# Chunked attention with a mixture of experts on one core: the second product turned for two batches, seven products one step sooner

## The chip, the core and the metric

The kernel runs on one core of a Trainium2 chip. What is measured is the time of one execution on the device, in microseconds (us). Three runs of the kernel before gave 1075.25, 1075.27 and 1075.59 us; their median is 1075.27.

## What is computed

Four batches of 768 tokens, 8 heads of 64: each chunk of 32 tokens attends to 8 memory keys and to its neighbourhood (16 tokens to the left, 8 to the right). The result, 3072 tokens x 512 features, goes through four experts, each with two matrix products, and the experts' outputs are added with routing weights:

```python
for c in range(nc):                       # chunks of 32
    k_full = np.concatenate([mem_k, k_ctx], axis=2)
    scores = scale * np.matmul(q_c, k_full.transpose(0, 1, 3, 2))
    a = np.exp(scores - np.max(scores, axis=-1, keepdims=True))
    a = a / (np.sum(a, axis=-1, keepdims=True) + 1e-09)
    out[:, :, c_start:c_end] = np.matmul(a, v_full)
...
p = domain_probs / (domain_probs.sum(-1, keepdims=True) + 1e-09)
for e in range(E):                        # 4 experts, w1: 512x1024, w2: 1024x512
    h = np.maximum(x @ w1[e], 0.0)
    out += p[:, e:e + 1] * (h @ w2[e])
```

## The kernel before

**Steps.** There are 16 steps, n = 4 x batch + expert. A step computes both products of one expert for the 768 tokens of one batch, in two halves of 384 tokens (SG). All operands are fp32 numbers split into a high and a low part; a product of two is three passes of TensorE (high x high, high x low, low x high). The splitting is a cast on ScalarE and a subtraction on VectorE or GpSimd (`parts_of`, L531).

**Seven products.** Where a product is cut into 2 x 2 blocks, `combine_x`, `make_pair` and `make2_combined` build sums of blocks so that seven block products do instead of eight. The first product has this form from step 1 on (classes `Pair` and `Full`: `one_two`, `six`, `five`, `seven`, `four`, `three`). Its seven products are done for four pairs of feature blocks p = 0 to 3, each a group of 6 matmuls of 384 columns (L860), with a weight block as the stationary operand and tokens as the columns. The second product is plain in steps 0 to 4 (`Tokens`, L822: 6 token tiles x 8 feature blocks x 3 passes = 144 matmuls of 512 columns, L840), and has seven products from step 5 (`Halves`, L1047: the hidden activations are the stationary operand, the columns are 256 output features, 3 token tiles per product; L1084). What it adds up in PSUM, `add_up` (L805) multiplies by the routing weight p_e of each token, a per-partition scalar there, and adds to `acc` in SBUF: on VectorE, with a first copy on ScalarE.

**Three stages.** The program is written in three plans. The first covers the attention of batch 0 and part of step 0; the second steps 0 to 4; the third steps 5 to 15. While a batch's experts run, the attention of the next batch is computed in between (`attend`, `window`), eight units a batch. In the second stage the first-layer weights of a step are loaded, combined, split, used, and stored in HBM (`make_pair`, L685); w2 likewise (`make2`); the combined w2 blocks (`make2_combined`, L746) are made from raw tiles and only stored. In the third stage nothing is split any more: `Stream` (L989) brings stored weights through a ring of 9 tiles of 512 KB, in order of use, and sends a load when a tile comes free.

**What sets the order.** `Plan` (L112) records every operation with its engine, a time from a formula, and the tiles it reads and writes. TensorE's order is as written; on the other engines and on SyncE, which issues all DMAs in order, a list scheduler orders by due time. `run` (L185) tries 100 variants (600 in the first stage), replays each, and keeps the best by TensorE's end, or by the last end in the last stage. Operations written with `join` may go to VectorE or GpSimd. `after` (L217) hands engine times on to the next plan; there SyncE may start up to 4 us ahead of it. At the end of the second stage the pools of raw tiles, weights and hidden tiles are closed and the ring is laid over them (`open_fin`, L423).

Of the kernel before, what the change touches and what calls it, by code (L numbers as in the profile page):

```python
# [38 lines left out]


# [19 lines left out]
DMA_ISSUE, DMA_FIRST, DMA_RATE = 0.45, 2.0, 345e3  # L60
ENGINES = ("PE", "ACT", "DVE", "POOL", "SP")
# [21 lines left out]
class Tile:  # L83
# [4 lines left out]
    def __init__(self, make, parts):  # L88
        self.make, self.parts, self._ap, self.ops = make, parts, None, []
        self.held, self.behind, self.born = False, None, 0  # L90
# [10 lines left out]
class Op:  # L101
# [3 lines left out]
    def __init__(self, engine, time, fn, birth, two, bytes_, index):  # L105
# [3 lines left out]
        self.floor = 0.0  # L109


class Plan:  # L112
# [21 lines left out]
    def slot(self, tag, aps, parts=1):  # L134

        t = self.tile(None, tag, len(aps), parts)
        t._ap = t.behind._ap if t.behind else aps[len(self.tags[tag]) - 1]
        return t
# [17 lines left out]
    def add(self, engine, time, fn, reads=(), writes=(), two=False, bytes_=0, other=None):  # L156
# [8 lines left out]
        for key in reads + writes:  # L165
            op.floor = max(op.floor, self.ends.get(key, 0.0))
            t = key[0] if isinstance(key, tuple) else key
            if isinstance(t, Tile):
                assert not getattr(t, "gone", False), "a tile is used after its place was given away"
                if t.behind is not None:  # L170
                    op.deps.update(t.behind.ops)
                    t.behind.gone = True
# [12 lines left out]
    def run(self, turns=TURNS, seed=1, last=False):  # L185

        ops, self.last = self.ops, last
# [83 lines left out]
    def replay(self, order, seed):  # L271
# [3 lines left out]
        dma = pool_to = dve_to = 0.0  # L275
# [21 lines left out]
        self.done = free  # L297
        return max(end) if self.last else free["PE"]

    def schedule(self, bias, ways):  # L300
# [10 lines left out]
        dma = pool_to = dve_to = drift = 0.0  # L311
# [77 lines left out]
PIECES = [[(0, KW, 0)], [(0, KW, CH)], [(0, NM, MEM), (NM, KW, 2 * CH + NM)]]  # L389
KORDER = [f for p in range(NP2) for f in (p, p + NP2)]  # L390
# [3 lines left out]
def tile_chunked_attention_moe(ctx: ExitStack, tc: tile.TileContext, qk, v, probs, w1, w2, out):  # L394
# [6 lines left out]
    opool = ctx.enter_context(tc.tile_pool(name="opool", bufs=6))  # L401
    mid_ctx = ExitStack()
    raw = mid_ctx.enter_context(tc.tile_pool(name="raw", bufs=3))
# [73 lines left out]
    psum_e = const.tile([P, NT, 1], F32, name="psum_e")  # L477

# [68 lines left out]
    def window(us, i, last=False):  # L547
# [71 lines left out]
        def inverted():  # L619
# [4 lines left out]
        dve(lambda: nc.vector.tensor_tensor(  # L624
            out=s_sb.ap, in0=s_sb.ap, in1=sm.ap.broadcast_to([UQ, H, KW]), op=ALU.mult), n_s, [sm], [s_sb])
# [12 lines left out]
    def combine_x(first):  # L638
# [6 lines left out]
        t3 = new(lambda: late["sb"], [P, h2 * SG + 256], "s_t", 1)  # L645
        t3_ap = lambda: t3.ap[:, 0:n_x].rearrange("p (a b) -> p a b", a=h2)

        def put(dst, name, i, x, key):
            at = slice(i * h2, (i + 1) * h2)
            parts_of(lambda: dst[0][:, at], lambda: dst[1][:, at], x, n_x, [key], (name, i, 0), (name, i, 1))  # L650

        def sub(out, x, y, reads, writes):
            join(out, x, y, ALU.subtract, n_x, reads, writes)

        if not first:
            put(xa, "xa", 0, lambda: b11, k11)
            put(xa, "xa", 1, lambda: b21, k21)
        sub(t3_ap, lambda: b22, lambda: b12, [k22, k12], [t3])
        if not first:
            put(xb, "xb", 1, lambda: b22, k22)  # L660
        sub(lambda: b12, lambda: b12, lambda: b11, [k11], [k12])
        sub(lambda: b22, lambda: b22, lambda: b12, [k12], [k22])
        put(xc, "xc", 1, lambda: b22, k22)
        put(xc, "xc", 0, lambda: b12, k12)
        put(xc, "xc", 2, t3_ap, t3)
        sub(lambda: b21, lambda: b21, lambda: b22, [k22], [k21])
        put(xb, "xb", 0, lambda: b21, k21)
# [11 lines left out]
    def want_pair(n, p):  # L679
        r = new(lambda: late["sb"], [P, 2 * DM], "raw_pair", 2, parts=2)  # L680
        for i, f in enumerate((p + NH, p)):
            dma(lambda i=i: r.ap[:, i * DM:(i + 1) * DM], lambda f=f: w1[n % E, f], P * DM * 4, [], [(r, i)])
# [829 lines left out]
```

## Time and profile before

| | us |
|---|---|
| median of three runs | 1075.27 |
| the profiled execution | 1075.24 |
| its span, first to last instruction | 1073.5 |
| TensorE busy | 1057.2 |
| VectorE / ScalarE / GpSimd busy | 757.1 / 651.5 / 305.2 |

The page of the profile also shows a mean DMA rate of 267 GB/s, and three of 40 slices in which TensorE is busy for less than nine tenths: the first (6), the fifteenth around 380 us (8), where the second stage ends, and the last (8). Matmuls overlap in the records, so the time from one start to the next tells what one costs.

### The profile page before, as it was taken

What the parts mean: (1) busy time and instruction counts of PE and PEld (TensorE: products, weight loads), DVE (VectorE), ACT (ScalarE), POOL (GpSimd) and SP (SyncE); (2) the same over time, 40 slices, a digit from 0 to 9 for tenths busy, and PEclk for the clock granted to TensorE, in tenths of its full rate; (3) what the DMA queues carried; (4) which work ended last, traced back from release to release, by engine and by line L of the source; (5) the groups of instructions that cost most, each with busy time, mean ns of one, the idle gap of its engine ahead of it and who ended that gap; (6) DMA issues with size and microseconds to landing.
All of it is one profiled execution on the core that took longest, in us unless ns stands there. A gap on an engine that the chain in (4) does not pass through costs nothing.

```text
span 1073.5 us, 20388 instructions
## 1 busy us (share of the span) xinstructions
PE 1057.2 (98%) x7438; PEld 1010.7 (94%) x7438; DVE 757.1 (71%) x1366; ACT 651.5 (61%) x1654; POOL 305.2 (28%) x302
## 2 busy tenths in 40 slices
PE   6999999999999989999999999999999999999998
PEld 6988988989889889999999999999999999999998
DVE  5956876757786348869698865858689654747474
ACT  5836885657665657585865867657592645435261
POOL 3321524627253214243352612112010221303020
PEclk8999999999999999999999999999999999999999
DMA  8553696967877499999998978878777977877783
GB/s 266 188 185 125 248 386 225 393 227 298 316 254 292 144 342 315 307 351 323 336 327 301 345 242 279 255 238 273 239 241 240 303 252 234 267 233 248 247 258 136
DMA packets 169364, 286.61 MB, mean 267 GB/s; under 512 B 14128, under 2 KB 108336, under 8 KB 169264
## 3 DMA queue, kind: packets, MB, share of 16 engines
q1 hardware_dynamic: 169264, 285.31, 77.8%
q8 instruction: 59, 0.97, 0.4%
q14 instruction: 41, 0.34, 0.1%
HBM read 216.06 MB, written 69.21 MB: 266 GB/s over the span
## 4 chain that ended last, share of the span: by engine, by line
PE 97%; DVE 1%; ACT 1%; DMA 1%; POOL 0%; issue 0%; SPq 0%; POOLq 0%; ACTq 0%; DVEq 0%
PE a_ps L860 24%; PE a_ps L1084 18%; PE moe_ps L860 18%; PE moe_ps L840 14%; PE moe_ps L1084 13%; PE moe_ps L794 3%; PE s_ps L560 2%; PE x_ps L579 2%; PE att_ps L1249 1%; PE x_ps L1268 1%; PE x_ps L1148 1%; DMA ring<-k 0%; PE att_ps L1177 0%; ACT s_sb L615 0%; DMA t<-s_t 0%
## 5 line engine op out<-in xcount | busy, mean ns | idle before, releaser
L840 PE MATMUL moe_ps<-w,h_hi 128*128 128x512 f32 x480 | 149.6, 393 | 0.0
L521 DVE TENSOR_TENSOR u<-moe_ps,u 128x384 f32<-128x384 f32 x120 | 66.5, 555 | 79.3 <-PE moe_ps L860 61.1
L840 PEld LDWEIGHTS moe_ps<-w,h_hi 128*128 128x128 f32 x480 | 88.9, 188 | 18.7
L505 ACT ACTIVATE u<-u 128x384 f32<-128x384 f32 x132 | 68.8, 523 | 60.7 <-DVE u L521 60.5
L503 ACT COPY u<-a_ps 128x384 f32<-128x384 f32 x120 | 57.3, 477 | 73.2 <-PE a_ps L860 69.5
L522 POOL TENSOR_TENSOR u<-u,u 128x384 f32<-128x384 f32 x33 | 40.1, 1217 | 198.5 <-DVE us L521 194.7
L840 PE MATMUL moe_ps<-w,h_lo 128*128 128x512 f32 x240 | 93.8, 391 | 0.0
L521 DVE TENSOR_TENSOR A_lo<-u,A_hi 128x384 fp32r<-128x384 f32 x119 | 76.2, 649 | 18.6 <-ACT A_hi L503 18.4
L814 DVE SCALAR_TENSOR_TENSOR acc<-moe_ps,pr,acc 128x256 f32<-128x256 f32 (+1 forms) x109 | 56.7, 523 | 36.6 <-PE moe_ps L1084 21.8
L1084 PE MATMUL moe_ps<-ring,A_hi 128*128 128x256 f32 x440 | 80.9, 283 | 0.0
L814 DVE SCALAR_TENSOR_TENSOR acc<-a_ps,pr,acc 128x256 f32<-128x256 f32 x116 | 55.7, 480 | 35.3 <-PE a_ps L1084 34.5
L633 DVE STREAM_TRANSPOSE aT<-band 32x256 f32<-32x256 f32 x168 | 73.0, 435 | 5.6 <-ACT band L503 2.6
L860 PE MATMUL a_ps<-xc_hi,ring 128*128 128x384 f32 x352 | 75.6, 336 | 0.0
L522 POOL TENSOR_TENSOR u<-u,us 128x384 f32<-128x384 f32 x40 | 48.9, 1224 | 84.8 <-DVE A_lo L521 49.4
L1084 PEld LDWEIGHTS moe_ps<-ring,A_hi 128*128 128x128 f32 x440 | 69.0, 191 | 0.0
L503 ACT CAST A_hi<-u 128x384 fp32r<-128x384 f32 x132 | 67.4, 513 | 0.9
L1084 PE MATMUL a_ps<-ring,Sa_hi 128*128 128x256 f32 x352 | 65.4, 285 | 0.0
L615 ACT ACTIVATE s_sb<-s_sb,mx 96x64 f32<-96x64 f32 x192 | 64.5, 337 | 0.8
L1084 PE MATMUL a_ps<-ring,Sb_hi 128*128 128x256 f32 x352 | 64.8, 283 | 0.0
L1084 PE MATMUL a_ps<-ring,A_hi 128*128 128x256 f32 x352 | 64.6, 283 | 0.0
L860 PEld LDWEIGHTS a_ps<-xc_hi,ring 128*128 128x128 f32 x352 | 62.3, 188 | 0.0
L1084 PE MATMUL moe_ps<-ring,A_lo 128*128 128x256 f32 x220 | 62.2, 283 | 0.0
(214 smaller groups left out, 3000.0 us busy)
## 6 DMA issues: line engine op xcount, KB each, us to landing
ring<-k SPq DMA_DIRECT2D x132, 512.0 KB, 4.9
ring<-t SPq DMA_DIRECT2D x88, 512.0 KB, 5.6
ring<-w SPq DMA_DIRECT2D x66, 512.0 KB, 5.1
k<-w SPq DMA_DIRECT2D x48, 512.0 KB, 5.2
w<-w SPq DMA_DIRECT2D x40, 512.0 KB, 6.2
raw<-in_w_dram SPq DMA_DIRECT2D x62, 256.0 KB, 5.7
ring<-k SPq DMA_DIRECT2D x44, 256.0 KB, 4.5
qk_t<-in_qk_dram SPq DMA_DIRECT2D x24, 448.0 KB, 5.5
```

The lines of the kernel that those rows point to most:

```text
L503: nc.scalar.copy(out(), x())
L505: nc.scalar.activation(out(), x(), func)
L521: ("DVE", t_dve(cols), lambda: nc.vector.tensor_tensor(out=out(), in0=x(), in1=y(), op=op)),
L522: ("POOL", t_pool(cols), lambda: nc.gpsimd.tensor_tensor(out=out(), in0=x(), in1=y(), op=op)),
L560: nc.tensor.matmul(s_ps.ap[0:UQ, j * NPAIR + g, :], lhsT=qk_t.ap[rows, g * UQ:(g + 1) * UQ], rhs=qk_t.ap[rows, NPAIR * UQ + g * P:NPAIR * ...
L615: now["plan"].add("ACT", t_act(KW) + 0.01, lambda h=h: nc.scalar.activation(s_sb.ap[:, h, :], s_sb.ap[:, h, :], AF.Exp, bias=mx.ap[:, h, : ...
L633: dve(lambda c=c, kb=kb: nc.vector.transpose(out=aT[kb * CH:(kb + 1) * CH, :, c * CH:(c + 1) * CH], in_=band[c * CH:(c + 1) * CH, :, kb * ...
L794: nc.tensor.matmul(ps.ap[:, lo:hi], lhsT=a[:, c * P:(c + 1) * P], rhs=x[:, c, lo:hi], start=(i == 0), stop=(i == len(steps) - 1),)
L814: dve(lambda: nc.vector.scalar_tensor_tensor(out=o.ap[:, cols], in0=ps_ap(), scalar=p_e, in1=o.ap[:, cols], op0=ALU.mult, op1=ALU.add), n_ ...
L840: nc.tensor.matmul(self.ps.ap, lhsT=h.ap[:, self.rows], rhs=w.ap[:, part, :], start=(i == 0 and k == 0), stop=(i == NF - 1 and k == 2),)
L860: nc.tensor.matmul(ps.ap[:, 0:SG], lhsT=a()[:, c * P:(c + 1) * P], rhs=y[:, k0 + c, :], start=(first and i == 0), stop=(i == len(steps) - ...
L1084: nc.tensor.matmul(ps.ap[:, cols], lhsT=x.ap[:, rows], rhs=w_ap[:, y, :], start=(begins and k == 0 and i == 0), stop=(k == NP2 - 1 and i = ...
```

## The change

Parts:

- **Turned product.** In steps 8 to 15 (`FLAT = 2` batches on) class `Across` takes the place of `Halves`: the weight block is the stationary operand and the 384 tokens of a half are the columns. There are 2 feature tiles per product instead of 3 token tiles. The sums (`sum_tile`) lie in the block of memory of the former `acc` tiles, features across partitions; the output of these batches is stored transposed, and turned back by the host as a layout.
- **Routing ahead.** With features on partitions the routing weight is no per-partition scalar, so the hidden activations are multiplied by it. The weights are turned by TensorE once and stored (`lay_routes`); each step loads them, repeated over 128 partitions (`want_routes`). In pairs 2 and 3 and in block "12" one VectorE operation does relu and weight (`weigh`); elsewhere ScalarE's relu is followed by a multiplication on GpSimd or VectorE.
- **Seven products from step 4.** Step 4 leaves the second stage and becomes a `Full` step of the third. Its first-layer weights are made in steps 1 to 3, one pair a step and one more at the end of step 3; combined w2 blocks are made earlier (2 in each of steps 0 to 3, 2, 2 and 4 in steps 4 to 6; before 1, 1, 1 and 4 in steps 1 to 4, then 2, 3, 2, 2).
- **Sums in place.** `make2_combined` writes its sums into the raw tiles; `combine_x` overwrites its inputs; `make_pair` lays its sums in another order.
- **Queue ahead.** `LEAD = 7`: SyncE and the DMA engines may start a plan up to 7 us ahead, and the second stage's variants are charged for a SyncE that ends less than 7 us before TensorE. Two outputs of batch 0 are issued in the third stage.

The diff, cut to its core:

```diff
+FLAT = 2
...
+LEAD = 7.0
...
+        self.floor = -LEAD
...
+    def run(self, turns=TURNS, seed=1, last=False, ahead=None):
...
     def after(self, keys=()):
         zero = self.done["PE"]
-        free = {e: max(-4.0 if e == "SP" else 0.0, t - zero) for e, t in self.done.items()}
+        free = {e: max(-LEAD if e in ("SP", "DMA") else 0.0, t - zero) for e, t in self.done.items()}
         ends = {}
         for key in keys:
-            ends[key] = max([0.0] + [op.end - zero + LATENCY for op in self.writers.get(key, ())])
+            ends[key] = max([-LEAD] + [op.end - zero + LATENCY for op in self.writers.get(key, ())])
...
-        self.done = free
-        return max(end) if self.last else free["PE"]
+        self.done = {**free, "DMA": dma}
+        if self.last:
+            return max(end)
+        return free["PE"] + (max(0.0, free["SP"] + self.ahead - free["PE"]) if self.ahead else 0.0)
...
+SHARED = ()
+COMBINED_A = (2, 2, 2, 2)
+COMBINED_M = {4: 1, 5: 1, 6: 2}
+COMBINED_E = {4: 1, 5: 1, 6: 2}
+LAST = (2 * NTT - 2, 2 * NTT - 1)
+DIRECT = (2, 3)
...
-    def make2_combined(e, p):
...
+    def make2_combined(e, p, shared=False):
+        r0, r1 = (raws[e, f] if shared else want_raw(e, f) for f in (p, p + NH))
...
-        add(t1, b12, b11, ALU.subtract, [r0], 0)
-        add(t2, t1, b22, ALU.subtract, [r1, (t, 0)], 1)
-        add(t4, b21, t2, ALU.add, [r1, (t, 1)], 3)
-        add(t3, b22, b12, ALU.subtract, [r0, r1], 2)
-        for i in range(2):
-            x = lambda i=i: t.ap[:, i * DM:(i + 1) * DM]
-            keys = [(t, 2 * i), (t, 2 * i + 1)]
+        def add(out, x, y, op, reads, writes):
+            join(out, x, y, op, HQ, reads, writes, "POOL")
+        add(b11, b12, b11, ALU.subtract, [(r0, 1)], [(r0, 0)])
+        add(b12, b22, b12, ALU.subtract, [(r1, 1)], [(r0, 1)])
+        add(b22, b11, b22, ALU.subtract, [(r0, 0)], [(r1, 1)])
+        add(b21, b21, b22, ALU.add, [(r1, 1)], [(r1, 0)])
+        for i, r in enumerate((r0, r1)):
+            x = lambda r=r: r.ap
             hi = new(lambda: late["sb"], [P, DM], "t_hi", 1, F32R)
...
+        def weigh(self, u, x, half, keys, psum=False):
+            r = self.routes[half]
+            dve(lambda: nc.vector.scalar_tensor_tensor(
+                out=u.ap, in0=x(), scalar=0.0, in1=r.ap, op0=ALU.max, op1=ALU.mult),
+                SG, [r], [u] + keys, two=not psum)
+        def relu(self, u, half):
+            if self.routes and self.p in DIRECT:
+                self.weigh(u, lambda: u.ap, half, [])
+                return
             act(lambda: u.ap, lambda: u.ap, SG, [], [u], func=AF.Relu)
+            if self.routes:
+                r = self.routes[half]
+                join(lambda: u.ap, lambda: u.ap, lambda: r.ap, ALU.mult, SG, [r], [u], "POOL")
         def have(self, name, u):
-            self.relu(u)
+            self.relu(u, self.WHERE[name][1])
             if name == "11":
                 self.u11 = u
...
-            act(lambda: self.u12.ap, lambda: ps.ap[:, 0:SG], SG, [], [self.u12, ps], func=AF.Relu, psum=True)
+            if self.routes:
+                self.weigh(self.u12, lambda: ps.ap[:, 0:SG], 0, [ps], True)
+            else:
...
-            join(ap(s1), ap(self.u22), ap(u21), ALU.add, SG, [self.u22, u21], [s1])
-            join(ap(s2), ap(self.u11), ap(s1), ALU.subtract, SG, [self.u11, s1], [s2])
+            join(ap(s1), ap(self.u22), ap(u21), ALU.add, SG, [self.u22, u21], [s1], "POOL")
+            join(ap(s2), ap(self.u11), ap(s1), ALU.subtract, SG, [self.u11, s1], [s2], "POOL")
...
+    class Across(Halves):
+        STEPS = 2
+        def go(self, name, t):
+            left, right = self.WITH[name]
+            kind, half, col = self.INTO[name]
+            begins = kind == "c" or (kind, t) not in self.banks
+            if begins:
+                ps = bank("a" if kind == "a" else "moe")
+                if kind != "c":
+                    self.banks[kind, t] = ps
+                    ps.held = True
+            else:
+                ps = self.banks[kind, t]
+            rows = slice(t * P, (t + 1) * P)
+            for k in range(NP2):
+                w = self.stream.at[self.n, 2, right, k // 2]
+                hi, lo = self.k[k][left]
+                def fn(k=k, w=w, hi=hi, lo=lo):
+                    w_ap = w.ap.rearrange("p (k a b) -> p k a b", k=2, a=2)[:, k % 2]
+                    for i, (x, y) in enumerate(((hi, 0), (hi, 1), (lo, 0))):
+                        nc.tensor.matmul(
+                            ps.ap[:, 0:SG], lhsT=w_ap[:, y, rows], rhs=x.ap,
+                            start=(begins and k == 0 and i == 0), stop=(k == NP2 - 1 and i == 2),
+                            skip_group_check=True,
+                        )
+                pe(t_mm(SG, 3), fn, [hi, lo, w], [ps])
+            if name in "34":
+                ps.held = False
+            self.count[name] = self.count.get(name, 0) + 1
+            if self.count[name] == self.STEPS:
+                self.stream.done(*((self.n, 2, right, k) for k in range(2)))
+            key = self.n // E, half, 2 * col + t
+            fresh = key not in sums
+            if fresh:
+                sums[key] = sum_tile()
+            o = sums[key]
+            if fresh:
+                act(lambda: o.ap, lambda: ps.ap[:, 0:SG], SG, [ps], [o], psum=True)
+            else:
+                join(lambda: o.ap, lambda: ps.ap[:, 0:SG], lambda: o.ap, ALU.add, SG, [], [ps, o], psum=True)
+            if self.e == E - 1 and name in "2347":
+                dma(lambda: out_d[self.n // E - FLAT, 2 * col + t][:, half * SG:(half + 1) * SG], lambda: o.ap,
+                    P * SG * 4, [o], [("out", key)])
     written = set()
+    out_d = out[FLAT * S:].rearrange("n d -> (n d)").rearrange("(b c p t) -> b c p t", b=B - FLAT, c=NC, p=P)
+    sums, sum_places = {}, []
+    def sum_tile():
+        if len(sum_places) < 2 * NC:
+            i = len(sum_places)
+            t = now["plan"].have(acc_block[:, i * SG:(i + 1) * SG])
+            t.over = tuple(x for tok, x in accs.items() if tok // (2 * NTT) == FLAT - 1)
+            sum_places.append(t)
+        else:
+            old = sum_places.pop(0)
+            t = now["plan"].have(old.ap)
+            t.behind = old
+            sum_places.append(t)
+        return t
+    def want_routes(n, half):
+        t = new(lambda: late["fin"], [P, SG], "routes", 2)
+        b, e = divmod(n, E)
+        first = (2 * b + half) * NTT
+        rows = lambda: pr_dram.rearrange("(n e) t -> e n t", e=E)[e, first:first + NTT]
+        dma(lambda: t.ap.rearrange("p (n t) -> p n t", t=P), lambda: rows().partition_broadcast(P), P * SG * 4, [], [t])
+        return t
     places = {b: [(4 * b - 1, "B")] + [(4 * b + e, k) for e in range(3) for k in "AB"] for b in range(1, B - 1)}
...
+    order = [(n, p) for n in range(1, E) for p in range(NP2)]
+    for n in range(1, E):
+        order.insert(order.index((n, NP2 - 1)) + 1, (E, n - 1))
+    order.append((E, NP2 - 1))
...
+    def lay_routes():
+        rows = head.tile([E * NT, P], F32, name="pr_rows")
+        turned = x_bank[0:E * NT, DM - P:DM]
+        pe(0.1, lambda: nc.tensor.transpose(turned, pr.rearrange("p n e -> p (n e)"), ident), ["pr"], ["pr_t"])
+        moved(lambda: rows, lambda: turned, P, ["pr_t"], ["pr_rows"])
+        dma(lambda: pr_dram, lambda: rows, N * E * 4, ["pr_rows"], ["pr_dram"])
...
     combine_x(True)
...
-    for n in range(1, E + 1):
-        for f in KORDER[0:0]:
-            make2(n, f)
+    for n in range(1, E):
...
+            second_weights(n, p)
+            next_pair(*((n, p + 1) if p + 1 < NP2 else (E, n - 1)))
...
-        combine_some((1, 1, 1, 4)[n - 1])
+        combine_some(COMBINED_A[n])
...
-        next_pair(n + 1, 0)
+        next_pair(*((n + 1, 0) if n + 1 < E else (E, NP2 - 1)))
         tiles[2].go()
         tiles[3].go()
         attend(n, "B")
-        next_pair(n + 1, 1)
+        if n + 1 < E:
+            next_pair(n + 1, 1)
...
-        plan.run()
+        plan.run(ahead=LEAD)
...
+    keys += [(1, 0, p, i) for p in range(NP2) for i in range(4)]
...
+    plan = now["plan"] = Plan(free, ends)
+    for tok in range(2 * NTT):
+        accs[tok] = plan.have(accs[tok].ap, "acc", 2, [ends[accs[tok], i] for i in range(2)])
+        if tok in LAST:
+            give(tok)
...
-    stream = Stream(range(E + 1, B * E))
+    stream = Stream(range(E, B * E))
     rest = None
-    for n in range(E + 1, B * E):
+    for n in range(E, B * E):
         operands = [{} for _ in range(NP2)]
         pairs = []
-        second = Halves(n, operands, pairs, stream)
+        across = n >= FLAT * E
+        second = (Across if across else Halves)(n, operands, pairs, stream)
+        routes = [want_routes(n, half) for half in range(2)] if across else None
...
             elif rest:
-                rest.go("3", 2)
+                rest.go("3", rest.STEPS - 1)
...
-                combine_some({6: 1, 7: 2, 8: 2}.get(n, 0))
+                combine_some(COMBINED_M.get(n, 0))
...
-        combine_some({5: 2, 6: 2}.get(n, 0))
-        for name, t in (("1", 2), ("1", 1), ("2", 0), ("2", 1), ("5", 0), ("2", 2), ("5", 1), ("5", 2)):
-            second.go(name, t)
+        combine_some(COMBINED_E.get(n, 0))
+        for word in ("11 20 21 50 51" if across else "12 11 20 21 50 22 51 52").split():
+            second.go(word[0], int(word[1]))
...
+        for word in ("70 71 40 41 30" if across else "70 71 72 40 41 30 42 31").split():
+            second.go(word[0], int(word[1]))
...
-    return r.results[0]["out_0_dram"]
+    o = r.results[0]["out_0_dram"]
+    rows = FLAT * S
+    return np.concatenate([o[:rows], o[rows:].reshape(B - FLAT, DM, S).transpose(0, 2, 1).reshape(-1, DM)])
```

## Rows read from the trace of the kernel before

**Rows 1.** The page's busy table: us, share of the span, instructions.

```profile
PE 1057.2 (98%) x7438; PEld 1010.7 (94%) x7438; DVE 757.1 (71%) x1366; ACT 651.5 (61%) x1654; POOL 305.2 (28%) x302
```

**Rows 2.** Waits of TensorE and for what: total us, times, longest.

```profile
PE a_ps L860 <- DMA ring<-k: 4.0, 1, 4.0
PE att_ps L1249 <- POOL band L522: 3.2, 1, 3.2
```

**Rows 3.** TensorE in time, step 12: start, us, operation, count [idle before].

```profile
871.93 0.40 PE L1084 MATMUL moe_ps<-ring,Sa_hi 128*128 128x256 f32 x2
...
873.37 0.40 PE L1084 MATMUL a_ps<-ring,Sb_hi 128*128 128x256 f32 x2
```

**Rows 4.** The same view, first product of step 12.

```profile
852.03 0.87 PE L860 MATMUL moe_ps<-xa_hi,ring 128*128 128x384 f32 x4
...
853.10 0.87 PE L860 MATMUL a_ps<-xb_hi,ring 128*128 128x384 f32 x4
...
855.20 0.85 PE L860 MATMUL moe_ps<-xc_hi,ring 128*128 128x384 f32 x4
...
856.24 0.87 PE L860 MATMUL moe_ps<-xb_hi,ring 128*128 128x384 f32 x4
```

**Rows 5.** The same view, plain second product of step 0.

```profile
99.27 0.62 PE L840 MATMUL moe_ps<-w,h_hi 128*128 128x512 f32 x2
...
99.95 0.62 PE L840 MATMUL moe_ps<-w,h_hi 128*128 128x512 f32 x2
```

**Rows 6.** SyncE's DMA issues in order of time, where the second stage ends.

```profile
379.05 0.32 SPq L529 DMA_DIRECT2D t<-s_t  x1
379.41 5.69 SPq L529 DMA_DIRECT2D ring<-k  x9
```

**Rows 7.** TensorE in order of time, where the third stage begins.

```profile
384.81 1.65 PE L860 MATMUL a_ps<-xa_hi,ring 128*128 128x384 f32 x4 [4.01 <-DMA ring<-k]
...
388.45 0.86 PE L860 MATMUL a_ps<-xc_hi,ring 128*128 128x384 f32 x4
```

**Rows 8.** Stretches: busy of PE, PEld, DVE, ACT, POOL; clock; DMA share; GB/s.

```profile
107.30:308.80 201.50, 201.50 (x1164) 180.12 (x1161) 147.77 (x254) 139.98 (x381) 93.63 (x92) 1.00 0.78 289
187.00:207.00 20.00, 20.00 (x116) 20.00 (x115) 15.17 (x26) 14.57 (x33) 13.05 (x11) 1.00 1.02 388
384.80:449.60 64.80, 64.79 (x478) 63.88 (x479) 49.88 (x90) 41.41 (x112) 19.70 (x19) 0.98 0.98 342
386.00:387.00 1.00, 1.00 (x5) 1.00 (x4) 0.00 (x0) 0.00 (x0) 0.00 (x0) 0.50 1.02 414
830.60:890.30 59.70, 59.70 (x423) 59.70 (x422) 34.45 (x58) 31.42 (x69) 11.00 (x10) 1.00 0.82 269
```

**Rows 9.** Instructions on tile u: count, ns min/median/max, first and last start.

```profile
L521 DVE TENSOR_TENSOR u<-moe_ps,u x120: 501/558/559, 109.8 to 1041.1; 128x384 f32<-128x384 f32 x120
...
L521 DVE TENSOR_TENSOR Sb_lo<-u,Sb_hi x38: 542/549/2209, 435.8 to 1058.8; 128x384 fp32r<-128x384 f32 x38
...
L522 POOL TENSOR_TENSOR u<-u,u x33: 1015/1327/1398, 400.3 to 1043.1; 128x384 f32<-128x384 f32 x33
```

**Rows 10.** TensorE in order of time, last pair of step 12.

```profile
859.77 0.87 PE L860 MATMUL a_ps<-xb_hi,ring 128*128 128x384 f32 x4
860.48 0.51 PE L860 MATMUL a_ps<-xb_lo,ring 128*128 128x384 f32 x2
...
861.87 0.40 PE L1084 MATMUL moe_ps<-ring,A_hi 128*128 128x256 f32 x2
```

**Rows 11.** DMA issues: tiles, queue, count, KB each, median us to landing.

```profile
k<-w SPq DMA_DIRECT2D x48, 512.0 KB, 5.2
...
raw_pair<-in_w_dram SPq DMA_DIRECT2D x32, 256.0 KB, 5.2
t<-t_hi SPq DMA_DIRECT2D x32, 256.0 KB, 4.7
```

**Rows 12.** Instructions on tile pr, columns as in group 9.

```profile
L480 DVE TENSOR_REDUCE psum_e<-pr x1: 253/253/253, 64.5 to 64.5; 128x24 f32<-128x96 f32 x1
```

More of the change, by code (lines that the diff above doesn't have):

```diff
@@ L89, in __init__ @@
         self.make, self.parts, self._ap, self.ops = make, parts, None, []
-        self.held, self.behind, self.born = False, None, 0
+        self.held, self.behind, self.over, self.born = False, None, (), 0
     @property
@@ L183, in add @@
         self.ops.append(op)
-    def run(self, turns=TURNS, seed=1, last=False):
-        ops, self.last = self.ops, last
+    def run(self, turns=TURNS, seed=1, last=False, ahead=None):
+        ops, self.last, self.ahead = self.ops, last, ahead
         for op in ops:
@@ L806, in add_up @@
         if tok not in accs:
-            accs[tok] = new(lambda: opool, [P, DM], "acc", 6, parts=2)
+            accs[tok] = now["plan"].slot("acc", acc_tiles, 2)
         o = accs[tok]
@@ L1135, in fixed @@
         return [pool.tile([P, DM], F32, name=name, bufs=many) for _ in range(many)]
[L1137 to L1140 removed]
+    spots = fixed(early, "spot", 11 - RAWS)
+    acc_block = opool.tile([P, 6 * DM], F32, name="acc")
+    acc_tiles = [acc_block[:, i * DM:(i + 1) * DM] for i in range(6)]
+    raw_spots = fixed(raw, "raw", RAWS) + acc_tiles[:3] + spots[6:]
+    s_spots = [t[0:UQ].rearrange("p (h k) -> p h k", h=H) for t in spots[:6]]
     x_bank = ps_x.tile([P, DM], F32, name="x_ps")
@@ L1411, in tile_chunked_attention_moe @@
     with tc.manual_schedule():
-        plan.run()
+        plan.run(ahead=LEAD)
     open_fin()
-    plan = now["plan"] = Plan(*plan.after(
-        ["pr"] + [(name, i, part) for name, k in (("xa", 2), ("xb", 2), ("xc", 3)) for i in range(k) for part in range(2)]
-    ))
-    for tok, t in list(accs.items()):
-        if tok // (2 * NTT) == 1:
-            accs[tok] = plan.have(t.ap, "acc", 2)
-    us, i = windows[E + 1, "A"]
+    keys = [(name, i, part) for name, k in (("xa", 2), ("xb", 2), ("xc", 3)) for i in range(k) for part in range(2)]
+    keys += [(1, 0, p, i) for p in range(NP2) for i in range(4)]
+    keys += [("t2", e, i, p, part) for e in range(E) for i in range(2) for p in range(NP2) for part in range(2)]
+    keys += [(accs[tok], i) for tok in range(2 * NTT) for i in range(2)]
+    free, ends = plan.after(keys)
+    plan = now["plan"] = Plan(free, ends)
[3 more added lines that the diff above has]
+            give(tok)
+    us, i = windows[E, "A"]
     s = late_st[us[i - 1]]
@@ L1458, in tile_chunked_attention_moe @@
             combine_x(False)
-        for t in range(NTT):
+        for t in range(second.STEPS):
             second.go("6", t)
```

146 lines of the change are left out of this document (69 added, 77 removed).

## The prediction

> **What bounds the kernel now.** The first view is the page's busy table: TensorE is busy 1057.2 of the 1073.5 us span [rows 1], so the kernel is a queue of matrix products, and an edit counts through the products that it removes or the idle time that it opens or closes on this engine. The second view is TensorE's list of waits. From step 1 to the end it has one entry, 4.0 us on a ring tile's DMA; the others are the attention in front [rows 2]. So VectorE, ScalarE, GpSimd and the DMA queue set nothing today outside that place. The third view is TensorE's order of time, read for the distance from start to start, since the busy times of overlapping matmuls can't be added.
>
> - 256 columns wide (second product, seven-product form): a product of 12 matmuls from 871.93 to 873.37, 0.120 us each [rows 3].
> - 384 columns wide (first product): four products of 6 matmuls from 852.03 to 856.24, 0.1754 each; single products vary from 1.04 to 1.07, so from 0.1733 to 0.1783 [rows 4].
> - 512 columns wide (plain second product): 3 matmuls from 99.27 to 99.95, 0.2267 each [rows 5].
>
> The profiled execution took 1075.24 us, 1.74 more than its span; the median of the runs is 1075.27, so sums on the profiled time can be set against the median as they stand.
>
> **The turned second product (steps 8 to 15).** Before: 7 products x 3 token tiles x 4 pairs x 3 passes = 252 matmuls of 256 columns, 252 x 0.120 = 30.24 us a step. After: 7 x 2 x 4 x 3 = 168 of 384, 168 x 0.175 = 29.40 us. The columns are equal in number, 64,512; what goes is 84 times the fixed part of a matmul. Gain 0.84 a step, 6.7 in eight steps. With 0.1733 it would be 9.0, with 0.1783 2.3. That a turned matmul takes what the first product's takes (same width and type, a ring tile as weights) is the assumption.
>
> **Step 4 in seven products.** 144 x 0.2267 = 32.64 us become 30.24: 2.4 us gained; with 0.001 us more or less on either width 2.0 to 2.8.
>
> **The change of stage.** Before, SyncE issued the last store of the combined weights at 379.05 and the first ring load only behind it, at 379.41 [rows 6]; TensorE stood idle for 4.01 us until 384.81 [rows 7]. It then ran at a granted clock of 0.50, the 1.2 of its two levels in GHz [rows 8]: the two products up to 388.45 took 3.64 us [rows 7] against 2.10 at the full level. Together 4.01 + 3.64 - 2.10 = 5.5 us. After, the plan is charged for a DMA queue that ends less than LEAD = 7 us ahead of TensorE, the last stage of it holds two combinations where it held four, the last two outputs are sent later, and the ring may be planned from 7 us ahead. A ring load of before lands 5.4 us after its issue (379.41 to 384.81), so 7 us cover the first. What can keep it late: ring tiles lie where raw tiles and first-layer weights lay, and both are now in use late (combinations are made in the raw tiles; the last two pairs made are step 4's). I take 5.0 of the 5.5, the rest being a short wait; bounds 0 and 5.5.
>
> **Added work on other engines.** In steps 8 to 15 the relu of the two DIRECT pairs and of every "12" block goes from ScalarE to VectorE with the routing weight in one operation: 10 a step at the 0.558 of the nearest row = 5.6 us [rows 9]. The accumulations go from 21 narrower to 14 of that length, which I count as even. VectorE so has some 6 us more in steps where it was busy 34.45 of 59.7 [rows 8]. GpSimd gets 6 multiplications and the sums by default, at 1.327 [rows 9]: below half busy. Neither becomes the bound; TensorE's products hide them. If that cover went, some 6 us a step would show. The queue gets two small loads of routing weights a step, in place of nothing, at a DMA share of 0.82.
>
> **One new wait.** The turned product needs a PSUM bank of its own for each accumulator, so product 1 of the second row block takes the bank that the last pair's product four has just filled, with only product three between. Step 12 of before shows the distances: product four runs from 859.77, its last matmuls end at 860.48 + 0.51 = 860.99, and what stands behind product three starts at 861.87 [rows 10]. In the new order the emptying is VectorE's weighing: 860.99 + 0.56 = 861.55, which leaves some 0.3 us for the handing over and for what VectorE is just doing. Behind that wait stand all further products. A VectorE operation usually lasts 0.55 us, but one on two SBUF operands was stretched to 2.209 [rows 9]; the emptying itself reads PSUM, and of that kind none of 120 took over 0.559. So 0 to 1.9 us a step, 0 to 15 in all; nearest the median row is 0.1 a step. I take 0.8 in all.
>
> GpSimd's operations and the stretched row: the Trainium skill says in "SBUF — State Buffer", Who interferes with whom, that a VectorE operation with two SBUF inputs and a GpSimd operation that reads SBUF lock each other out whole, whichever comes second waiting to the end, and that one with a single SBUF input doesn't take part. By that rule, with more GpSimd work in these steps, an operation ahead of the weighing would more often last 0.55 + 1.33 us, and eight such waits would cost 8 x 1.6 = 13 us; the trace agrees with the kind that is stretched, and by its medians with few of them.
>
> **Steps 1 to 3 do more.** Step 4's weights of the first layer are made there, and combinations go from 3 to 6 between 107 and 309 us (two more in step 0). A pair of weights is two raw pieces of 256 KB and kept pieces, three of 512 KB [rows 11] and one half as wide, 2.36 MB; two of the four were already made in this stretch, so +4.7 MB. A combination is two pieces of 256 KB in and four out [rows 11], 1.57 MB; +4.7 MB. With the 58.2 MB of before (201.5 us at 289 GB/s) and the early ring's 4.7 that is 72 MB in some 207 us: 349 GB/s. The same stretch shows 20 us at 388 with a share of 1.02 and TensorE never idle, while step 5 shows 342 at 0.98 [rows 8]. So the demand comes to 0.90 to 1.0 of what the queue moved. At 388 nothing shows; at 342, 72 MB take 211 us and the stage ends 4 us later, with single late weights up to 12. VectorE, 147.8 of 201.5 us here, gets 2 pairs and 3 combinations, some 12 us. I take 1.5 us, bounds 0 and 12.
>
> **The rest.** In the first stage TensorE now turns the routing weights ahead of the first token tile, at about 55 us: one transpose, 0.1 to 0.2 us. It needs VectorE's four routing operations, which ran from 64.5 on [rows 12] and must now run 10 us sooner; they last about 1 us and VectorE is not full there. I take 0.2, bounds 0 and 1.5. The sums in place (combined weights, inputs) have as many operations on the same tile sizes, hidden behind the second product; taken at nothing, between -0.5 and 0.5. The tail stays: one addition and one store of 192 where 256 KB stood.
>
> Sum: 1075.24 - 6.7 - 2.4 - 5.0 + 0.8 + 1.5 + 0.2 = 1063.6 us. The gains at their largest give 1075.24 - 9.0 - 2.8 - 5.5 = 1057.9.
>
> **Rivals.**
> 1. The stage change keeps its stall: SyncE ends early in the plan, but the raw tiles come free only with the last stores, and ring loads wait behind that. For it: the last store of before went out 0.4 us ahead of the ring. Against: two combinations less. 1063.6 + 5.0 = 1068.6.
> 2. The bank wait of product 1 decides: the weighing stands each time behind an operation stretched to some 1.4 us (between the ends of [rows 9]), 8 x 1.1 = 9 us in place of 0.8: 1071.9. Against: the medians, and that the plan can put the emptying first. By the rule from the Trainium skill's "SBUF — State Buffer" above it would be up to 1063.6 - 0.8 + 13 = 1075.8; the medians leave that 0.02 of this rival's chance.
> 3. The first-layer weights starve steps 1 to 3, and the kernel is slower. It decides when the queue moves less than about 330 GB/s there, or when a store that waits for its sum holds the loads behind it, once a step, as long as the one of [rows 7]. Each such stall then costs the 4.0 us of [rows 2] and the 1.5 of the slow clock: 3 x 5.5 = 16.5 in place of 1.5, 1078.6. For it: the sum of bytes above, three raw tiles with two held longer by each combination. Against: 20 us at a full queue without a wait.
> 4. The turn does nothing: if matmuls with ring weights take 0.1783, or banks are waited for so often that the fixed part comes back, 2.3 instead of 6.7: 1068.0.
>
> **From these to the numbers.** Forecast (all three gains, 1059 to 1067) 0.66; rival 1 0.12; rival 2 0.07; rival 3 0.11; rival 4 0.04. What can be told from no change is 0.2%, 2.2 us: under 1073.1 faster, over 1077.4 slower. Rivals 1 and 4 are faster, rival 2 mostly (0.05 of 0.07), rival 3 is slower with 0.08 and between with 0.03: faster 0.87, same 0.05, slower 0.08. The range 1058.5 to 1071.5 holds the forecast but for its edges, rivals 1 and 4 and half of rival 2, 0.83 in all.
>
> **What will show it.** Turned products that start 2.10 us apart (12 matmuls), and steps 12 to 14 of 58.8 us instead of 59.6; a first ring load issued 5 us or more before the last 512-wide matmul, and a clock of 1.00 behind it; TensorE's waits without an entry over 1 us in steps 1 to 3. Wrong it is if TensorE waits in those steps for raw pieces or weights, if product 1's second block waits for VectorE over 0.3 us in most steps, or if turned matmuls lie further apart than 0.178 us.

## The result, and the profile after

The changed kernel takes 1060.99 us (median of 5 runs, 1059.87 to 1064.36) against 1075.27: a ratio of 0.9868, 95% interval 0.9852 to 0.9885, so 14.3 us less. Forecast were 1063.6 us, 1058.5 to 1071.5. A second set of the same kernel gave 1061.48 beside 1075.98, a ratio of 0.9870 (0.9855 to 0.9884). The profiled execution took 1059.87, the shortest of the five.

The page after, its span and busy table (against [rows 1]):

```profile
span 1058.1 us, 19540 instructions
## 1 busy us (share of the span) xinstructions
PE 1045.8 (99%) x6875; PEld 1002.5 (95%) x6875; DVE 801.0 (76%) x1339; ACT 632.4 (60%) x1599; POOL 486.4 (46%) x448
```

TensorE is busy 11 us less and the span 15.4 us shorter, so 4 us of idleness went as well. VectorE and GpSimd have 44 and 181 us more. TensorE's list of waits (total us, times, longest), without the attention in front but for its longest row:

```profile
PE att_ps L1366 <- issue: 2.8, 1, 2.8
...
PE moe_ps L812 <- DVE h_lo L798: 0.4, 1, 0.4
PE a_ps L1162 <- DVE u L978: 0.4, 1, 0.4
...
PE a_ps L878 <- ACT u L525: 0.3, 1, 0.3
```

The row on the ring's DMA [rows 2] is gone. In its place stand three of 0.3 to 0.4 us: the one on `h_lo` in step 0, the one on VectorE's `u` in step 13, the last in step 7. Where the time went is read from five matmuls: the first on block "11" of steps 1, 3, 6 and 8, and the last one of all (start, us, operation, count), before and then after:

```profile
107.34 0.62 PE L860 MATMUL a_ps<-xa_hi,w 128*128 128x384 f32 x2
...
242.24 0.51 PE L860 MATMUL a_ps<-xa_hi,w 128*128 128x384 f32 x2
...
449.65 0.51 PE L860 MATMUL a_ps<-xa_hi,ring 128*128 128x384 f32 x2
...
577.10 0.51 PE L860 MATMUL a_ps<-xa_hi,ring 128*128 128x384 f32 x2
...
1069.39 0.28 PE L1084 MATMUL moe_ps<-ring,Sb_lo 128*128 128x256 f32 x1
```

```profile
105.88 0.62 PE L878 MATMUL a_ps<-xa_hi,w 128*128 128x384 f32 x2
...
240.78 0.51 PE L878 MATMUL a_ps<-xa_hi,w 128*128 128x384 f32 x2
...
439.72 0.51 PE L878 MATMUL a_ps<-xa_hi,ring 128*128 128x384 f32 x2
...
567.88 0.51 PE L878 MATMUL a_ps<-xa_hi,ring 128*128 128x384 f32 x2
...
1054.12 0.34 PE L1162 MATMUL moe_ps<-Sb_lo,ring 128*128 128x384 f32 x1
```

| stretch | before | after | difference |
|---|---|---|---|
| to step 1 | 107.34 | 105.88 | -1.5 |
| steps 1 and 2 | 134.90 | 134.90 | 0.0 |
| steps 3 to 5, with the change of stage | 207.41 | 198.94 | -8.5 |
| steps 6 and 7 | 127.45 | 128.16 | +0.7 |
| steps 8 to 15, to the last matmul | 492.29 | 486.24 | -6.05 |

The 0.7 us of steps 6 and 7 are two short pauses in step 7: against the same matmuls of before, TensorE is 0.51 us late from 506.25 us on and another 0.20 from 545.35 on.

**The turned product.** Its groups of 12 matmuls, in order of time:

```profile
868.86 0.51 PE L1162 MATMUL a_ps<-A_hi,ring 128*128 128x384 f32 x2
...
870.94 0.51 PE L1162 MATMUL a_ps<-A_hi,ring 128*128 128x384 f32 x2
...
873.02 0.51 PE L1162 MATMUL moe_ps<-Sb_hi,ring 128*128 128x384 f32 x2
```

2.08 us for 12, so 0.1733 us each, where a matmul of 256 columns has 0.120 [rows 3].

**The change of stage.** SyncE's last store of step 3 and the first ring load behind it, and TensorE at the start of step 4:

```profile
305.96 0.34 SPq L551 DMA_DIRECT2D out_dram<-acc  x1
306.39 5.27 SPq L551 DMA_DIRECT2D ring<-k  x9
```

```profile
312.56 0.39 PE L858 MATMUL moe_ps<-w,h_lo 128*128 128x512 f32 x1
312.79 0.86 PE L878 MATMUL a_ps<-xa_hi,ring 128*128 128x384 f32 x4
...
314.87 0.86 PE L878 MATMUL a_ps<-xc_hi,ring 128*128 128x384 f32 x4
```

The ring's first load still follows a store by some 0.4 us, but both now go out early: the load 6.4 us ahead of step 4, and TensorE doesn't stand. Before, it was 5.4 us ahead of a start that it held up by 4.0 [rows 6, 7]. The last 512-wide matmul and the first ring matmul are 0.23 us apart, and two products take 2.08 us: no wait, no low clock.

**Steps 1 to 3.** The stretches, columns as in [rows 8]; the rows are step 1, step 12 and steps 1 to 3:

```profile
105.90:174.40 68.50, 68.50 (x411) 61.14 (x410) 53.79 (x94) 55.10 (x159) 37.87 (x37) 1.00 0.93 338
...
817.20:876.20 59.00, 58.89 (x338) 58.57 (x337) 43.38 (x62) 25.38 (x56) 27.32 (x23) 1.00 0.85 275
105.90:305.00 199.10, 199.10 (x1152) 178.18 (x1151) 161.83 (x269) 145.42 (x384) 105.90 (x104) 1.00 0.91 335
```

In steps 1 to 3 the DMA share rose from 0.78 to 0.91 (335 GB/s), VectorE's busy share from 0.73 to 0.81, and TensorE was busy all the time, as before. In step 12 VectorE is busy 43.4 us, where it had 34.5 [rows 8].

**The new wait.** Step 13, product four from 906.86, product three from 907.92, then product 1's second row block; TensorE, then VectorE, then GpSimd:

```profile
907.92 0.87 PE L878 MATMUL moe_ps<-xb_hi,ring 128*128 128x384 f32 x4
908.62 0.51 PE L878 MATMUL moe_ps<-xb_lo,ring 128*128 128x384 f32 x2
909.52 0.62 PE L1162 MATMUL a_ps<-A_hi,ring 128*128 128x384 f32 x2 [0.38 <-DVE u L978]
```

```profile
907.16 1.37 DVE L978 SCALAR_TENSOR_TENSOR u<-u,routes 128x384 f32<-128x384 f32 x1
908.45 0.54 DVE L543 TENSOR_TENSOR acc<-a_ps,acc 128x384 f32<-128x384 f32 x1
908.92 0.54 DVE L978 SCALAR_TENSOR_TENSOR u<-a_ps,routes 128x384 f32<-128x384 f32 x1
```

```profile
906.85 1.26 POOL L544 TENSOR_TENSOR us<-u,u 128x384 f32<-128x384 f32 x1 [1.89 <-DVE u L978]
908.19 1.21 POOL L544 TENSOR_TENSOR us<-u,us 128x384 f32<-128x384 f32 x1
```

VectorE's emptying of the bank (908.92, 0.54 us) stands behind a weighing on two SBUF operands that lasted 1.37 us, beside GpSimd's sum of 906.85 to 908.11, and behind one accumulation, which takes 0.47 us from start to start. TensorE starts 0.55 us late (product three takes 1.05 us, [rows 4], so the next was due at 908.97), and its next matmul is another 0.11 us late. In steps 12 and 15, with 0.28 and 0.30 us, the emptying stands straight behind a stretched subtraction of 1.37 us: 1.4 us in all, in three of eight steps.

Whether GpSimd goes with the stretching can be counted over the whole trace. Of VectorE's 411 operations of this size (128x384, fp32) on two SBUF operands, 182 lasted over 0.7 us, and each of the 182 overlaps one of GpSimd's; of the other 229, 52 do, and they kept to 0.63 us at most. Of the 340 that read PSUM, 176 overlap one, and none lasted over 0.561 us.

### The profile page after: what moved, and what is told of

Read it like the earlier page. It is cut to its first block, busy times and chain, and to the rows that moved or that the text cites. A ratio compares the mean times of both kernels' runs of the same rounds, so it can differ in the third digit from the quotient of the medians.

```text
span 1058.1 us, 19540 instructions
## 1 busy us (share of the span) xinstructions
PE 1045.8 (99%) x6875; PEld 1002.5 (95%) x6875; DVE 801.0 (76%) x1339; ACT 632.4 (60%) x1599; POOL 486.4 (46%) x448
## 4 chain that ended last, share of the span: by engine, by line
PE 87%; DVE 5%; DMA 4%; ACT 2%; issue 1%; POOL 0%; SPq 0%; DVEq 0%; POOLq 0%; ACTq 0%
PE a_ps L878 21%; PE moe_ps L878 16%; PE a_ps L1162 12%; PE moe_ps L858 12%; PE moe_ps L1162 9%; PE a_ps L1118 5%; PE moe_ps L1118 4%; PE moe_ps L812 3%; PE s_ps L582 2%; PE x_ps L601 2%; DMA t<-raw 2%; DVE A_lo L543 2%; DVE u L978 1%; DMA raw<-in_w_dram 1%; DVE u L543 1%
## 5 line engine op out<-in xcount | busy, mean ns | idle before, releaser
L544 POOL TENSOR_TENSOR u<-u,routes 128x384 f32<-128x384 f32 x44 | 48.0, 1091 | 193.0 <-ACT u L527 193.0
L543 DVE TENSOR_TENSOR A_lo<-u,A_hi 128x384 fp32r<-128x384 f32 x133 | 113.8, 870 | 14.9 <-ACT A_hi L525 14.5
L858 PE MATMUL moe_ps<-w,h_hi 128*128 128x512 f32 x384 | 119.8, 393 | 0.0
L544 POOL TENSOR_TENSOR raw<-raw 128x256 f32<-128x256 f32 x62 | 57.1, 923 | 73.6 <-DMA raw<-in_w_dram 42.5
L544 POOL TENSOR_TENSOR us<-u,u 128x384 f32<-128x384 f32 x48 | 54.9, 1144 | 68.2 <-ACT u L527 36.5
L1162 PE MATMUL a_ps<-A_hi,ring 128*128 128x384 f32 x256 | 65.3, 335 | 0.6 <-DVE u L978 0.4
L525 ACT COPY band<-s_sb 32x512 f32<-32x512 f32 (+2 forms) x100 | 49.0, 510 | 14.7 <-DVE s_sb L543 10.3
L525 ACT COPY s_sb<-s_ps 32x64 f32<-32x64 f32 (+2 forms) x96 | 44.6, 465 | 20.4 <-PE s_ps L582 19.3
L544 POOL TENSOR_TENSOR us<-u,us 128x384 f32<-128x384 f32 x45 | 52.1, 1158 | 4.6 <-DVE Sb_lo L543 1.5
L544 POOL TENSOR_TENSOR w<-raw,w 128x512 fp32r<-128x512 f32 x23 | 33.8, 1471 | 39.7 <-ACT w L525 38.9
```

The costliest lines, as they stand in the source:

```text
L525: nc.scalar.copy(out(), x())
L543: ("DVE", t_dve(cols), lambda: nc.vector.tensor_tensor(out=out(), in0=x(), in1=y(), op=op)),
L544: ("POOL", t_pool(cols), lambda: nc.gpsimd.tensor_tensor(out=out(), in0=x(), in1=y(), op=op)),
L858: nc.tensor.matmul(self.ps.ap, lhsT=h.ap[:, self.rows], rhs=w.ap[:, part, :], start=(i == 0 and k == 0), stop=(i == NF - 1 and k == 2),)
L1162: nc.tensor.matmul(ps.ap[:, 0:SG], lhsT=w_ap[:, y, rows], rhs=x.ap, start=(begins and k == 0 and i == 0), stop=(k == NP2 - 1 and i == 2), ...
```

## The experiments

All are the changed kernel with the edit shown, four to six executions each. "Product 2 between", "no queue ahead", "four combinations late" and "no turn" ran beside runs of before of 1075.62 us, the others, on another chip, beside 1075.98. With every edit to the program the random search found a new order for the plans that it touches, so a difference is read by stretch, in the steps that the edit concerns. The changed kernel once more, with no edit, on the chip of the second group:

> The changed kernel once more, on the chip of the next three, so that they can be set against it. Expected: the ratio of before, 0.987 within 0.0015, no stall at the start of step 4, and again pauses of TensorE ahead of product 1's second block in some of the eight turned steps, in all 1 to 2 us.

Measured: 1061.48 us, ratio 0.9870; no stall at step 4; pauses of 0.13, 0.38 and 0.13 idle us at product 1's second block in steps 12, 13 and 15. Two things differed from the first profile: step 1 began at 107.32, not 105.88, and step 7 took 64.01 us, not 64.50, because the pause at 506.25 was missing.

**Product 2 between product 1's blocks.**

```diff
-            for word in ("11 20 21 50 51" if across else ...
+            for word in ("20 11 21 50 51" if across else ...
```

> The changed kernel with one thing different: in the turned steps the first row block of product 2 stands between product 1's two row blocks (order 20 11 21 50 51). Theory: the three pauses of TensorE ahead of product 1's second block (0.275, 0.545 and 0.297 us, each with some 0.11 at the restart, 1.4 us together in steps 12, 13 and 15) come from the bank that VectorE empties late, behind an operation stretched to 1.37 us; with 3.1 us instead of 1.05 between, all three go: 1061.0 - 1.4 = 1059.6. Rival: VectorE is late there as a whole, and the pause moves to product 2, whose operands come from the same block: 1061.0 within 0.5.

Measured: 1061.33 us (1061.10 to 1065.40), ratio 0.9876 (0.9859 to 0.9893). The rival held: no gain. The pauses at product 1 are gone, but product 2 waits for its own operand, the low part of block 12. In the profiled execution (the longest of the four, 1065.40 us), step 13:

```profile
912.66 0.58 PE L1162 MATMUL moe_ps<-A_hi,ring 128*128 128x384 f32 x2
915.13 0.44 PE L1162 MATMUL moe_ps<-A_lo,ring 128*128 128x384 f32 x1 [1.90 <-DVE A_lo L543]
```

```profile
908.88 1.37 DVE L978 SCALAR_TENSOR_TENSOR u<-u,routes 128x384 f32<-128x384 f32 x1
910.18 1.37 DVE L543 TENSOR_TENSOR A_lo<-u,A_hi 128x384 fp32r<-128x384 f32 x1
...
912.52 1.30 DVE L978 SCALAR_TENSOR_TENSOR u<-u,routes 128x384 f32<-128x384 f32 x1
913.74 1.34 DVE L543 TENSOR_TENSOR A_lo<-u,A_hi 128x384 fp32r<-128x384 f32 x1
```

Four stretched operations on VectorE, with two short ones between the second and the third, make the operand 1.9 us late. In this execution the granted clock then fell to its lower level for 3.4 us, and step 13 took 62.45 us against 59.49 in the changed kernel, while step 12 took 58.65 against 58.99.

**No queue ahead.**

```diff
-        self.floor = -LEAD
+        self.floor = 0.0
...
-        plan.run(ahead=LEAD)
+        plan.run()
```

and the other places of LEAD likewise as before the change.

> The changed kernel without the queue ahead: plans may start SyncE 4 us early and nothing else, the ring is planned from 0, and the second stage is not charged for a late SyncE. Everything else stays (two combinations in step 3, two outputs sent later). Theory: without the charge the ring's first load goes out late again, TensorE stands for 2 to 4 us at the start of step 4 and then runs 1.5 us longer at the low clock: 1064 to 1067. Rival: the end of the second stage simply holds less work for the queue; then no stall and 1061 within 1.

Measured: 1065.77 us, ratio 0.9912 (0.9899 to 0.9926). The theory held in the time, not in the clock: TensorE's wait for the ring is back, in two parts, but the granted clock stays at its full level behind them. SyncE's first ring load goes out only 1.4 us ahead of the time at which step 4 could begin (0.23 us behind the start of the last 512-wide matmul, here at 313.25), against 6.4 in the changed kernel:

```profile
PE a_ps L878 <- DMA ring<-k: 3.4, 2, 1.9
```

```profile
311.67 0.34 SPq L551 DMA_DIRECT2D out_dram<-acc  x1
312.11 5.57 SPq L551 DMA_DIRECT2D ring<-k  x9
```

**Only the charge taken away.**

```diff
-        plan.run(ahead=LEAD)
+        plan.run()
```

> The changed kernel with only the charge for a late SyncE taken from the second stage's search; the ring may still be planned from 7 us ahead. Theory: the charge is what moves the last stores forward (306.4 for the first ring load with the whole queue ahead, 312.1 without it), so TensorE waits 2 to 4 us at the start of step 4 and the time is 3 to 6 us longer. Rival: the freedom to start ahead does it, and the time stays within 1 us of the changed kernel.

Measured: 1064.93 us, ratio 0.9903 (0.9888 to 0.9918), 3.45 more than the changed kernel beside it. The theory held. The first load goes out 2.6 us ahead of the time at which step 4 could begin (the last 512-wide matmul starts at 312.77), so the freedom to start ahead moves it by 1.2 us against the kernel without any of it, and the charge by 3.8 more:

```profile
PE a_ps L878 <- DMA ring<-k: 2.4, 2, 1.4
```

```profile
310.39 5.79 SPq L551 DMA_DIRECT2D ring<-k  x9
```

Steps 3 and 4 together are 3.1 us longer than in the changed kernel beside it, of which 2.4 are this wait. The new order also left single pauses of 0.3 to 0.7 us in the third stage, while step 1 of this execution began 1.2 us sooner.

**Four combinations late.**

```diff
-COMBINED_A = (2, 2, 2, 2)
+COMBINED_A = (2, 1, 1, 4)
```

> The changed kernel with the combinations of w2 blocks at 2, 1, 1 and 4 in steps 0 to 3 instead of 2 each: four late ones in the second stage's last step, as in the kernel before. Theory (the charge for a late SyncE keeps the ring on time): within 1 us of 1061, since the plan moves the stores forward. Rival (what went is due to less work at the end): the stall is back, 1064 to 1067. If the bytes in steps 1 to 3 cost anything, fewer combinations in steps 1 and 2 would show there as a gain.

Measured: 1071.83 us, ratio 0.9966 (0.9954 to 0.9979): 10 us more than the changed kernel, worse than either theory said. With the charge in place the stores still come last, the first ring load goes out at 315.78, and TensorE stands for 7.2 us (SyncE in order of time; then the stretches of the wait and after it):

```profile
313.68 0.32 SPq L551 DMA_DIRECT2D t<-raw  x1
314.93 0.34 SPq L551 DMA_DIRECT2D out_dram<-acc  x1
315.78 5.08 SPq L551 DMA_DIRECT2D ring<-k  x9
```

```profile
312.20:319.50 7.30, 0.14 (x1) 0.00 (x0) 5.75 (x11) 3.91 (x20) 0.00 (x0) 0.69 0.84 294
319.50:323.50 4.00, 3.99 (x12) 3.99 (x13) 2.37 (x6) 1.47 (x3) 0.00 (x0) 0.50 0.93 346
```

Behind the wait the granted clock is 0.50 for as long as the window shows. By the trace it was at the lower level for 10.2 us, from 314.9 to 325.2; 4.6 of these lie in the wait, and the 5.6 behind it at half the clock cost some 2.8 us. With the wait of 7.2 that makes the 10 us. So the even spread of the combinations is needed at least as much as the charge. Steps 1 and 2, with one combination less each, took the same 68.50 and 66.40 us, so their bytes cost nothing at this load.

**No turn.**

```diff
-FLAT = 2
+FLAT = 4
...
-        across = n >= FLAT * E
+        across = False
...
-                lay_routes()
```

> The changed kernel without the turned product: all batches in the form with 256 columns, routing weights applied at the sum, and without the transpose of the routing weights in the first stage; step 4 and the queue ahead as in the change. Theory: the turn gave 6.0 us from the start of step 8 to TensorE's end, so steps 12 to 14 take 59.6 again, and 1061.0 + 6.0 = 1067.0 with step 1 starting at 105.9 us; if the 1.5 us of the first stage came only because the added transpose led the plan's search another way, step 1 starts at 107.3 as before, and the time is 1068.5. Rival: the waits and the added VectorE work ate the turn, then 1061 to 1063.

Measured: 1069.32 us, ratio 0.9939 (0.9926 to 0.9951): 0.7% more than the changed kernel (0.9939 - 0.9868 = 0.0071, 7.6 us). By stretch the turn's share is less: from the start of step 8 to the last matmul it is 492.28 us against 486.24, so 6.0. Steps 4 to 7 lost 2.2 us with pauses of 1.2 and 0.5 that the new order left there. Steps 12 and 13 take 59.6 us again:

```profile
825.03:884.64 59.61, 59.61 (x421) 59.61 (x421) 30.00 (x50) 30.84 (x68) 18.12 (x16) 1.00 0.80 265
884.64:944.26 59.62, 59.62 (x421) 59.62 (x421) 33.25 (x57) 25.72 (x56) 21.71 (x20) 1.00 0.76 245
```

Step 1 begins at 107.27, as in the kernel before; but so it does, at 107.32, in the changed kernel run again, so this doesn't tell what the added transpose does to the search.

**All weighing on VectorE.**

```diff
-DIRECT = (2, 3)
+DIRECT = (0, 1, 2, 3)
```

> The changed kernel with the weighing of all four pairs on VectorE in one operation (DIRECT = 0, 1, 2, 3); GpSimd loses 6 multiplications a turned step and ScalarE 6 relus. Theory: the operations ahead of the weighing are stretched by GpSimd's sums of the last pair, not by its multiplications (these belong to pairs 0 and 1), so the pauses stay as they are: within 1 us of the changed kernel. Rival: any relief of GpSimd shortens VectorE's stretched operations; then the pauses (1.4 us) go. Other rival: VectorE, with 6 more operations a step, becomes late: 2 us or more slower.

Measured: 1064.12 us, ratio 0.9894 (0.9878 to 0.9911), 2.6 more than the changed kernel. TensorE's waits on VectorE:

```profile
PE a_ps L1162 <- DVE u L978: 1.4, 3, 0.8
...
PE a_ps L1118 <- DVE Sa_lo L543: 0.5, 1, 0.5
```

The theory missed, and neither rival held whole: in steps 12 to 15 the pauses went (58.61 to 58.64 us for each of 12 to 14), and in steps 9 to 11, where attention runs beside, three new ones of 0.25 to 0.82 us came. About 2 us more were lost in steps 4 to 7, in whose operations the edit changes nothing: there the order that the search found differs. So this one does not tell the cause apart.

**Another bank.**

```diff
-                ps = bank("a" if kind == "a" else "moe")
+                ps = bank("a" if kind + str(t) in ("a0", "b1") else "moe")
```

> The changed kernel with one PSUM bank exchanged in the turned steps: the second accumulator of products 1, 6, 7, 4 lies in a bank of the other pool, and the second one of products 5, 3 takes the bank that product four fills, four products later. The order of products stays. Theory: the pauses ahead of product 1's second block come from that bank alone, so they go and nothing takes their place: 1.0 to 1.5 us faster than the changed kernel. Rival: as when product 2 was put between, VectorE's lateness shows at the next product instead: no gain.

Measured: 1058.93 us (1058.02 to 1059.49), ratio 0.9845 (0.9830 to 0.9860), 2.55 less than the changed kernel beside it, whose runs begin at 1060.84. No wait of the turned products is left, and steps 12 and 13 take 58.6 us with VectorE as busy as in the changed kernel:

```profile
818.03:876.64 58.61, 58.61 (x337) 58.61 (x337) 42.70 (x63) 26.45 (x56) 23.61 (x20) 1.00 0.84 275
876.64:935.26 58.62, 58.62 (x338) 58.62 (x338) 40.65 (x64) 21.94 (x46) 25.66 (x22) 1.00 0.79 259
```

From the start of step 8 to the last matmul it needs 2.0 us less than the changed kernel beside it (569.10 to 1053.33 against 568.82 to 1055.08). This version beats both kernels.

Not all of it is the bank. The emptying usually starts 0.38 us behind the start of product four's last matmul; in the changed kernel it came at 0.91, 1.18 and 0.93 us in steps 12, 13 and 15, and here, in an order found anew, at 0.38, 0.57 and 0.38. What the bank does shows in step 8, where the emptying came at 1.18 us (601.80 to 602.98) and product 1's second block, in its other bank, began on time (VectorE, then TensorE):

```profile
602.98 0.54 DVE L978 SCALAR_TENSOR_TENSOR u<-a_ps,routes 128x384 f32<-128x384 f32 x1
```

```profile
603.04 0.51 PE L1162 MATMUL moe_ps<-A_hi,ring 128*128 128x384 f32 x2
```

## Why the prediction was right, step by step

**The sum** came out 2.6 us too high; no term had the wrong sign but the first stage's. Short pauses in the rest of the third stage, 0.7 us in step 7, had no term.

- *The turn*, forecast -6.7, is -8.1 where nothing waits: 58.61 us a step (in the kernel with the other bank) against the 59.62 of the kernel without the turn. The term was mis-sized because I took the first product's mean distance, 0.175; turned matmuls keep to 0.1733, the lower end of [rows 4]. With that the prediction's own sum gives 9.0. In steps 12 and 13 of these two kernels the 504 narrow matmuls take 60.38 us from start to start and the 336 turned ones 58.26, which is 1.06 a step; the first product is 0.05 a step slower. That a matmul has a fixed part, and that 84 of them go, is shown: the groups of 12 take 2.08 us with 4,608 columns, and 18 matmuls of 256 columns, the same 4,608, need 18 x 0.120 = 2.16 [rows 3]. Of the 8.1, steps 8 to 15 show 6.05: the new wait takes 1.4, and matmul for matmul against the kernel with the other bank two more pauses, 0.33 us in step 8 (at 572.68) and 0.26 in step 13 (at 899.45), both in the first product, take the rest.
- *The new wait*, forecast +0.8, was +1.4, and by the mechanism named: the emptying behind a stretched operation. That it needs the bank is shown by step 8 of the kernel with the other bank; that the pauses of steps 12, 13 and 15 went there is in part the new order. That the stretching goes with GpSimd's work is shown by the count over the trace, where no stretched operation is without one of GpSimd's; the experiment on the weighing, where the order changed as well, doesn't tell. The Trainium skill's rule in "SBUF — State Buffer", Who interferes with whom, names the kind of operation that was stretched, 1.37 us against 0.54, and the reading from PSUM stayed at 0.54. The harder case that the prediction made of it, eight such waits, did not come, because in five steps the stretched operation lay elsewhere. In step 14 a subtraction of 1.37 us ended 0.29 us ahead of the emptying, so the small number of waits is in part luck of the order.
- *The change of stage*, forecast -5.0, gave all of the 5.5: steps 3 to 5 are 8.5 us shorter, which is 5.5 + 2.4 for *step 4* + 0.6. Of the 0.6 some 0.45 is step 4's again: the 512-wide matmuls of these steps lie 0.230 us apart (168 of them in 38.6 us), not 0.2267, so its 144 would have taken 33.1 us and not 32.64. No run leaves step 4 in its old form, so its term rests on these distances. The prediction named four causes of the earlier load and did not weigh them. The runs do: without the charge the wait is 2.4 us, without charge and freedom 3.4, and with four late combinations, charge and freedom kept, 7.2. The two outputs sent later were not tested alone.
- *Steps 1 to 3*, forecast +1.5, cost nothing, at a DMA share of 0.91. The bytes were summed rightly, 335 GB/s over 199.1 us or 66.7 MB against 72 less the early ring's 4.7. Rival 3 needed the queue to fall behind; it didn't.
- *Added work*: VectorE got 8.9 us in step 12 (43.4 against 34.5), not some 6; TensorE's products hid it but for the new wait.
- *The first stage*, forecast +0.2, came out at -1.5 in the profile. This is no gain of the change. Kernels with the same first stage started step 1 at 105.28 (four late combinations), 105.88, 106.09 (no charge), 107.32 and 108.00 us (product 2 between) in single executions; 105.88 and 107.32 are one and the same program. TensorE's routing transpose ran at 52.6 us, waited for nothing, and the next matmul began 0.07 us behind its start.

## What to carry to other kernels

On an engine that is already 98% busy, look for the fixed part of an instruction: fewer, wider matmuls with the same columns gain it, and here each operand's turn was paid by engines with room. The prefetch across the stage boundary needed freedom to start early, a plan that is charged for a late queue, and less work in the queue ahead of it; each kernel here that lacked the second, the first two, or the third had TensorE wait. When an order gives a PSUM bank back to TensorE after one product, count what may stand ahead of the emptying on its engine, stretched; here another order of products only moved the wait, and with another bank a late emptying held up nothing.

## What was unexpected

A short stop of TensorE costs more than its idle time: each of the three pauses of the changed kernel at product 1 was followed by a matmul some 0.11 us longer, and one pause of 1.9 us, with product 2 between, by 3.4 us at the lower clock, while the two of 1.9 and 1.5 us without the queue ahead, some 2 us apart, were followed by none. And a plan found by a random search carries some 2 us of chance: steps in whose operations the edit changes nothing took 0.4 to 0.7 us more each with all weighing on VectorE, and up to 1.8 more (step 5) without the turn, so experiments on such a kernel are better read by stretch than by their total. Some of it is not the plan's: the same program twice differed by 0.5 us in step 7 and by 1.4 in the start of step 1.
